# A spectral layer and two MLP layers on one core: who makes the low parts of the early weight pairs, and how the inverse transform's PSUM is cut

## The chip, the cores and the metric

The program runs on one core of one Trainium2 chip. Its time is the device time of one launch in microseconds, as the median of three runs. TensorE (PE) does the matrix products, VectorE (DVE), ScalarE (ACT) and GpSimd (POOL) the elementwise work, SyncE (SP) and POOL issue the DMAs.

## The reference

```python
X = np.fft.rfft(x, axis=1)                       # x: 2 x 3008 x 256
Yr = Xr @ w_r - Xi @ w_i + b_r
Yi = Xr @ w_i + Xi @ w_r + b_i
Y = soft_threshold(Yr, 0.01) + 1j * soft_threshold(Yi, 0.01)
x = np.fft.irfft(Y, n=3008, axis=1).reshape(6016, 256)
for w_in, w_out in ((moe_w_in, moe_w_out), (moe2_w_in, moe2_w_out)):
    h = x @ w_in                                 # 6016 x 2048
    x = (h * sigmoid(c * h)) @ w_out             # c = 1.702, then 1
```

The weights of the two MLP layers are float64 in memory. The kernel reads them as raw 64-bit words and makes float32 values of them on the chip.

## The kernel before

The program has four stages, one after the other on PE. **Forward** (16 tiles, `psf`): the input is folded into sums and differences and multiplied by cosine and sine matrices. **Middle** (12 tiles, `psm`): the complex product with `w_r` and `w_i`, then the threshold. **Inverse** (16 tiles, `psi`): for each parity q of the output index, each batch b and t = 0 to 3, the coefficients times a matrix. **MLP**: two layers, six blocks of 1024 (the last 896) tokens, eight groups each.

In the middle and in the MLP a float32 product is made of three products of a faster type: a number is cut into a high part (a cast) and a low part (the number less its high part), and high x high, high x low and low x high are added. `split` (L98) does this for weights: ACT casts, and POOL or DVE subtracts. For the middle's own input, `xsplit` (L470) makes the low part `xl` in another way: ACT writes minus the number in the faster type (L476), and a DMA issued by POOL adds the number onto it (L477). DMAs that add can be issued by POOL alone in this program.

**Weight pairs.** The weights come in 32 pairs of 128-row slices, in the order of `WEIGHTS` (L33): in 0 to 5, out 0 to 3, then out 4, in 6 and so on. One `tick` (L251) takes each pair one step on. It loads a pair (`raw`, one buffer, 512 KB), turns the bits of another (one operation on ACT, five on DVE, `cv_bits`, L159), sends the DMA that adds the two halves of the number (`cv_a<-cv_c`, L227), and places the one before that: `place_in` (L192) makes four sums on DVE in `tmp` (one buffer) and splits 384 and 512 columns; `place_out` (L183) splits 512. Ticks stand at listed steps: forward tiles 6, 9, 12, middle tiles 2, 6, 10, inverse tiles 1, 4, 7, 10; after that one in most MLP groups.

**Inverse.** Tiles t = 0, 1 of a (q, b) go into `rt`, tiles t = 2, 3 are added to and subtracted from it (L627, L628), and `inv_out` (L636) folds four times into `yt`, the MLP's input. Each tile has two PSUM banks, one for each half of the 128 + 128 channels; the four banks of one pool hold t = 0, 1 and the four of the other t = 2, 3. For q = 0, tiles t = 0, 1 are built of an even and an odd part: ACT copies the odd one to `eo` (L611, one buffer), and DVE makes sum and difference (L619, L374).

**Order.** In the inverse PE's instructions stand in the order of the code, and those of the other engines are put in order when the program is built, by a planned timeline; so are all engines' in the first MLP group. In the forward stage POOL and SP keep the order of the code, in the middle SP. Every engine runs its queue in order: an instruction that waits holds what is behind it.

Of the kernel before, what the change touches and what calls it, by code (L numbers as in the profile page):

```python
# [56 lines left out]
def spectral_mlp_kernel(ctx, tc, xin, mfwd, minv, wc, bias, w_in1, w_out1, w_in2, w_out2, outT):  # L57
# [101 lines left out]
    def cv_bits(raw):  # L159
# [875 lines left out]
```

## Time and profile before

| what | value |
|---|---|
| median of three runs | 1178.72 us (1176.81 to 1180.5) |
| the profiled execution: its own time, span | 1181.88 us, 1179.8 us |
| PE, PEld, DVE, ACT, POOL busy | 98%, 80%, 54%, 65%, 42% of the span |
| granted TensorE clock, mean | 0.998 of full speed |
| chain that ended last | 72% PE, 5% ACT, 2% DVE |

A busy PE is not PE at its peak, since its matmuls overlap. What counts is where it stands still, and for whom. A row of a timeline gives the start from the span's start, the length, the engine, the line of the kernel, the operation, output <- inputs and their shapes, the count, and in brackets the idle time ahead with the instruction that ended it. SP and POOL's DMA rows are the issue, not the transfer.

### The profile page before, as it was taken

How to read it: one execution, taken by the hardware profiler on the slowest of the kernel's cores; microseconds unless marked ns; L12 is line 12 of the kernel's file. 1: busy time of each engine (PE TensorE's matmuls, PEld its weight loads, DVE VectorE, ACT ScalarE, POOL GpSimd, SP SyncE). 2: the span in 40 equal slices, each digit the busy share in tenths (PEclk: the TensorE clock that was granted, in tenths of full speed). 3: DMA queues.
4: the chain of work that ended last, by engine and by line, in shares of the span. 5: the costliest groups of instructions: out<-in, count | busy, mean ns of one | idle time of the engine just before them, and what ended most of it. 6: DMA issues, size and time to landing. Idle time of an engine off the chain costs nothing.

```text
span 1179.8 us, 14452 instructions
## 1 busy us (share of the span) xinstructions
PE 1157.4 (98%) x5036; PEld 940.4 (80%) x5036; DVE 632.7 (54%) x976; ACT 761.3 (65%) x1437; POOL 499.9 (42%) x421
## 2 busy tenths in 40 slices
PE   7999989999999999999999999999999999999998
PEld 4758866788888888888889978878888888888897
DVE  7857998666456465565564553432532623524422
ACT  2465633678667667677667776666765765766655
POOL 2353532454444444444436755333333333433333
PEclk9999999999999999999999999999999999999999
DMA  7568332231221221121120100000000000000000
GB/s 267 181 135 229 54 72 54 55 80 28 54 72 36 54 72 28 45 72 37 54 63 28 54 18 19 1 37 1 1 37 1 20 17 1 36 1 1 36 1 32
DMA packets 33610, 61.35 MB, mean 52 GB/s; under 512 B 3073, under 2 KB 12289, under 8 KB 33538
## 3 DMA queue, kind: packets, MB, share of 16 engines
q1 hardware_dynamic: 25730, 46.28, 11.6%
q0 software_dynamic: 7808, 14.16, 6.9%
q8 instruction: 39, 0.64, 0.2%
q14 instruction: 33, 0.27, 0.1%
HBM read 35.92 MB, written 10.35 MB: 39 GB/s over the span
## 4 chain that ended last, share of the span: by engine, by line
PE 72%; ACT 5%; DVE 2%; issue 1%; DMA 0%; POOL 0%; DVEq 0%; ACTq 0%; POOLq 0%
PE o L727 38%; PE x L755 34%; ACT yt L758 2%; ACT g L760 1%; ACT x L674 1%; DVE x L681 1%; ACT yt L774 0%; DVE yt L776 0%; DVE yt L731 0%; DVE yt L797 0%; ACT yt L791 0%; DMA cv_a<-cv_c 0%; ACT yt L789 0%; ACT yt L731 0%; ACT wi L99 0%
## 5 line engine op out<-in xcount | busy, mean ns | idle before, releaser
L765 POOL TENSOR_TENSOR g<-yt,g 128x512 fp32r<-128x512 f32 (+1 forms) x282 | 361.3, 1294 | 531.6 <-PE x L755 364.3
L727 PE MATMUL o<-g,wo 128*128 128x512 f32 (+1 forms) x2304 | 561.0, 386 | 0.9 <-POOL g L765 0.9
L755 PE MATMUL x<-x,wi 128*128 128x512 f32 (+1 forms) x2016 | 501.7, 387 | 5.4 <-ACT yt L791 2.0
L727 PEld LDWEIGHTS o<-g,wo 128*128 128x128 f32 x2304 | 432.4, 188 | 83.6 <-POOL g L765 1.2
L755 PEld LDWEIGHTS x<-x,wi 128*128 128x128 f32 x2016 | 376.0, 188 | 86.0 <-ACT yt L774 5.6
L758 ACT ACTIVATE yt<-yt 128x512 f32<-128x512 f32 (+1 forms) x288 | 179.1, 622 | 257.8 <-DVE yt L797 209.9
L760 ACT CAST g<-yt 128x512 fp32r<-128x512 f32 (+1 forms) x384 | 234.4, 612 | 11.8
L797 DVE TENSOR_TENSOR yt<-yt,x 128x512 f32<-128x512 f32 (+1 forms) x96 | 64.7, 674 | 212.9 <-PE x L755 212.6
L776 DVE TENSOR_TENSOR yt<-yt,x 128x512 f32<-128x512 f32 (+1 forms) x96 | 64.8, 675 | 168.7 <-ACT yt L774 165.9
L765 DVE TENSOR_TENSOR g<-yt,g 128x512 fp32r<-128x512 f32 (+1 forms) x102 | 72.7, 713 | 77.8 <-ACT g L760 77.8
L344 PE MATMUL psf<-m,xf 128*128 128x376 f32 (+2 forms) x208 | 61.1, 456 | 6.4 <-DVE xf L303 6.1
L681 DVE TENSOR_TENSOR x<-yt,x 128x512 fp32r<-128x512 f32 (+1 forms) x46 | 47.8, 1038 | 36.1 <-ACT x L674 36.1
L800 DVE TENSOR_TENSOR yt<-yt,x 128x512 f32<-128x512 f32 (+1 forms) x96 | 64.7, 674 | 0.0
L344 PEld LDWEIGHTS psf<-m,xf 128*128 128x128 f32 x208 | 39.2, 199 | 27.6 <-DVE xf L303 7.3
L774 ACT COPY yt<-x 128x512 f32<-128x512 f32 (+1 forms) x96 | 54.7, 570 | 5.9 <-issue 3.6
L758 ACT ACTIVATE yt<-x 128x512 f32<-128x512 f32 (+1 forms) x96 | 56.1, 584 | 2.1 <-PE x L755 2.1
L344 PE MATMUL psi<-m,f 128*128 128x376 f32 (+3 forms) x208 | 52.1, 406 | 4.3 <-DVE rt L374 4.3
L791 ACT COPY yt<-x 128x512 f32<-128x512 f32 (+1 forms) x96 | 55.8, 581 | 0.8 <-PE x L755 0.8
L789 ACT COPY yt<-x 128x512 f32<-128x512 f32 (+1 forms) x96 | 54.8, 571 | 0.8 <-PE x L755 0.8
L344 PEld LDWEIGHTS psi<-m,f 128*128 128x128 f32 x208 | 37.2, 194 | 17.8 <-DVE rt L374 5.5
L227 POOL DMA_DIRECT2D cv_a<-cv_c x32 | 27.8, 870 | 24.7 <-DVE cv_c L174 14.2
L384 ACT COPY xt<-psf 128x128 f32<-128x128 f32 (+2 forms) x96 | 18.6, 282 | 28.6 <-PE psf L344 28.5
(99 smaller groups left out, 817.8 us busy)
## 6 DMA issues: line engine op xcount, KB each, us to landing
raw<-in_wi SPq DMA_DIRECT2D x32, 256.0 KB, 3.2
cv_a<-cv_c POOLq DMA_DIRECT2D x32, 256.0 KB, 3.3
raw<-in_wo SPq DMA_DIRECT2D x16, 512.0 KB, 3.4
raw<-in_x SPq DMA_DIRECT2D x12, 512.0 KB, 4.8
xl<-xt POOLq DMA_DIRECT2D x20, 256.0 KB, 7.6
out_t<-yt SPq DMA_DIRECT2D x20, 256.0 KB, 2.0
m<-in_mf SPq DMA_DIRECT2D x4, 564.0 KB, 5.3
m<-in_mi SPq DMA_DIRECT2D x4, 564.0 KB, 10.5
```

What stands on the lines that cost most here:

```text
L344: nc.tensor.matmul(ps, hi[:, c : c + P], m[:, k, :w], start=i == 0, stop=i == last)
L681: E('xl1' if l else 'xl0' if i == 0 else 'xl', k).tensor_sub(lo, src, r32(hi))
L727: nc.tensor.matmul(acc[h, mm], st, mv, start=first and k == 0, stop=last and k == 2)
L755: nc.tensor.matmul(ps, st, mv, start=first and m == 0, stop=m == 2, skip_group_check=True)
L758: nc.scalar.activation(g, g if src is None else src, func)
L760: nc.scalar.copy(gh, g)
L765: eng.tensor_sub(gl, g, r32(gh))
L776: nc.vector.tensor_add(y1, y1, Y)
L789: nc.scalar.copy(y2, Z)
L791: nc.scalar.copy(y3, X)
L797: nc.vector.tensor_add(y2, y2, X)
L800: nc.vector.tensor_add(y3, y3, Z)
```

## The change

- `split` gets a third way, `"D"`: ACT writes minus the number, POOL issues a DMA that adds the number, ACT casts the high part. `window` picks it for every pair that a tick places up to the last inverse tile (`outs[1]` is set behind it).
- Ticks stand at forward tiles 5, 8, 10, 13 (one more), middle tiles 3, 6, 9 and inverse tiles 0, 2, 5, 8. Pairs in 4 and later wait in `held` until the middle stage's buffers are closed; out pairs until inverse tile 5 (`po`).
- A tile of the inverse is one PSUM tile of two banks, four of them, in a pool of its own. ACT's copies and DVE's L627 and L628 take both halves in one instruction (L621, L641, L642 of the changed kernel).
- All folds of the threshold's result (`thf`, L530) are on DVE; one in four was on POOL.
- The buffer `a` of a conversion has three copies, and the weights fetched in the MLP use them too, where `ld` had one.

The entries that changed in the two tables of numbers are `thf`, `tf`, `tm`, `ti`, and the new `po`.

```diff
     def split(hi, lo, src, hi_eng=None, lo_eng=None):
+        if lo_eng == "D":
+            nc.scalar.mul(lo, src, -1.0)
+            nc.gpsimd.dma_start(out=lo, in_=src, accum_op=ALU.add)
+            nc.scalar.copy(hi, src)
+            return
...
-        a = cv_p.tile([P, 2 * CU], F32, tag="a", name="cv_a")
+        a = cv_p.tile([P, 2 * CU], F32, tag="a", name="cv_a", bufs=3)
...
     def window(k, done, now=False):
-        for u, a in done:
+        ready, held[:] = held + list(done), []
+        for u, a in ready:
+            if u[0] == "in" and u[2] >= NPR // 2 and not wib_p or u[0] == "out" and not outs[0]:
+                held.append((u, a))
+                continue
+            early = "D" if not now and not outs[1] else None
             if u[0] == "in":
-                sums, puts = place_in(u[1], u[2], a, E('pil', u[2]), sums_tmp)
+                sums, puts = place_in(u[1], u[2], a, early or E('pil', u[2]), sums_tmp)
...
-                place_out(u[1], u[2], a, E('pol', u[2]))
+                place_out(u[1], u[2], a, early or E('pol', u[2]))
...
-        a = cv_p.tile([P, 2 * CU], F32, tag="a" if kind == "in" else "ld", name="cv_ld", bufs=2 if kind == "in" else 1)
+        a = cv_p.tile([P, 2 * CU], F32, tag="a", name="cv_ld", bufs=3)
...
+    closed("ps1", "ps0")
+    psi_p = opened("psi", bufs=4, space=PS)
...
-        out = [bank(t // 2, "psi") for _ in range(2)]
+        pair = psi_p.tile([P, 2, 512], F32, tag="psi", name="psi")
+        out = [pair[:, x] for x in range(2)]
...
-        for mm in range(2):
-            r, a = row(rt[0], mm, t - 2, n), row(ac[0], mm, t - 2, n)
-            nc.vector.tensor_add(a, r, ps[mm][:, :n])
-            nc.vector.tensor_sub(r, r, ps[mm][:, :n])
+        r, a = rows(rt[0], t - 2, n), rows(ac[0], t - 2, n)
+        nc.vector.tensor_add(a, r, ps[:, :, :n])
+        nc.vector.tensor_sub(r, r, ps[:, :, :n])
...
+                outs[0] = step >= N('po')
...
+    outs[1] = True
     inv_post(*prev)
...
+    closed("psi")
+    ps_p[:] = [opened(f"ps{i}", bufs=4, space=PS) for i in range(2)]
```

The order of the instructions follows from the code and the planned timeline. Three places show it.

**POOL ahead of the middle's first split product.** `wi_` are the buffers of the placed in pairs, `xl<-xt_100` is the first low part that PE needs in the middle (its third tile). Before:

```order
L100 TENSOR_TENSOR wi_776<-cv_a,wi_776 128x384
L227 DMA cv_a<-cv_c 128x512
L100 TENSOR_TENSOR wi_776<-tmp,wi_776 128x512
L100 TENSOR_TENSOR wi_1012<-cv_a,wi_1012 128x384
L100 TENSOR_TENSOR wi_1012<-tmp,wi_1012 128x512
L227 DMA cv_a<-cv_c 128x512
L477 DMA xl<-xt_100 128x512
```

Now:

```order
L101 DMA wi_603<-cv_a 128x384
L101 DMA wi_603<-tmp 128x512
L232 DMA cv_a<-cv_c 128x512
L101 DMA wi_854<-cv_a 128x384
L101 DMA wi_854<-tmp 128x512
L101 DMA wi_1040<-cv_a 128x384
L232 DMA cv_a<-cv_c 128x512
L101 DMA wi_1040<-tmp 128x512
L487 DMA xl<-xt_100 128x512
```

Four in pairs are placed ahead of it (`wi_514` is further up) where there were three, and POOL's subtractions there have become DMAs. `tmp` has one buffer, and it is now read by a DMA: the next pair's sums wait until that DMA has landed.

**DVE in the inverse, second batch of q = 0.** L619 and L374 (now L634 and L384) read the tiles t = 0 and t = 1 whose banks PE needs again for q = 1; the numbers tell the tiles apart. Before:

```order
L619 TENSOR_TENSOR rt_1451<-psi_1401,eo_1452 128x2x2x95
L664 TENSOR_TENSOR tmp_1527<-yt_1325 128x512
L374 TENSOR_TENSOR rt_1451<-psi_1401,eo_1452 128x4x94
L665 TENSOR_TENSOR yt_1325<-yt_1325 128x512
L627 TENSOR_TENSOR ac_1480<-rt_1451,psi_1456 128x377
L681 TENSOR_TENSOR x_1604<-tmp_1527,x_1603 128x512
L627 TENSOR_TENSOR ac_1480<-rt_1451,psi_1457 128x377
L619 TENSOR_TENSOR rt_1451<-psi_1441,eo_1466 128x2x2x95
L628 TENSOR_TENSOR rt_1451<-rt_1451,psi_1456 128x377
L683 TENSOR_TENSOR tmp_1527<-yt_1325,tmp_1527 128x512
L170 TENSOR_SCALAR cv_c_1489<-cv_c_1489 128x512
L628 TENSOR_TENSOR rt_1451<-rt_1451,psi_1457 128x377
```

The next row there is L374 on `psi_1441`. Now:

```order
L634 TENSOR_TENSOR rt_1469<-psi_1444,eo_1470 128x2x2x95
L678 TENSOR_TENSOR tmp_1556<-yt_1349 128x512
L384 TENSOR_TENSOR rt_1469<-psi_1444,eo_1470 128x4x94
L679 TENSOR_TENSOR yt_1349<-yt_1349 128x512
L641 TENSOR_TENSOR ac_1514<-rt_1469,psi_1492 128x2x377
L642 TENSOR_TENSOR rt_1469<-rt_1469,psi_1492 128x2x377
L695 TENSOR_TENSOR x_1610<-tmp_1556,x_1609 128x512
L634 TENSOR_TENSOR rt_1469<-psi_1460,eo_1501 128x2x2x95
L175 TENSOR_SCALAR cv_c_1482<-cv_c_1482 128x512
L697 TENSOR_TENSOR tmp_1556<-yt_1349,tmp_1556 128x512
L384 TENSOR_TENSOR rt_1469<-eo_1501,psi_1460 128x4x94
```

The same work stands there in nearly the same order; two pairs of halves have become one instruction each, and the conversion's operation (L170, now L175) is still in it.

**DVE from the last inverse tile into the MLP.** The L648 rows (now L662) are the last `inv_out`, L776 (now L794) is the first sum of the MLP. Before:

```order
L627 TENSOR_TENSOR ac_1627<-rt_1600,psi_1619 128x376
L628 TENSOR_TENSOR rt_1600<-rt_1600,psi_1619 128x376
L627 TENSOR_TENSOR ac_1627<-rt_1600,psi_1620 128x376
L628 TENSOR_TENSOR rt_1600<-rt_1600,psi_1620 128x376
L648 TENSOR_TENSOR yt_1325<-ac_1627 128x2x376 x2
L648 TENSOR_TENSOR yt_1325<-rt_1600 128x2x376
L776 TENSOR_TENSOR yt_1325<-yt_1325,x_1645 128x512
L648 TENSOR_TENSOR yt_1325<-rt_1600 128x2x376
```

Now:

```order
L641 TENSOR_TENSOR ac_1630<-rt_1607,psi_1623 128x2x376
L642 TENSOR_TENSOR rt_1607<-rt_1607,psi_1623 128x2x376
L662 TENSOR_TENSOR yt_1349<-ac_1630 128x2x376 x2
L662 TENSOR_TENSOR yt_1349<-rt_1607 128x2x376 x2
L794 TENSOR_TENSOR yt_1349<-yt_1349,x_1651 128x512
```

The first sum has moved behind the fourth fold, and the last tile's fold is one wide instruction that starts only when both halves are there.

## Rows read from the trace of the kernel before

**Rows 1.** The waits of PE over the whole span: total us, times, longest

```profile
PE psi L344 <- DVE rt L374: 4.3, 2, 3.7
```

**Rows 2.** Windows: length, PE, PEld, DVE, ACT, POOL busy, clock, DMA share, GB/s

```profile
171.00:174.00 3.00, 2.55 (x6) 1.52 (x7) 3.00 (x7) 0.00 (x0) 0.00 (x0) 0.73 0.00 0
174.00:177.00 3.00, 3.00 (x8) 1.66 (x7) 3.00 (x6) 0.62 (x1) 0.00 (x0) 0.70 0.00 0
```

**Rows 3.** Timeline of PE in the inverse: start, us, line, tiles, idle before

```profile
160.10 3.02 PE L344 MATMUL psi<-m,f 128*128 128x190 f32 x12
163.71 4.06 PE L344 MATMUL psi<-m,f 128*128 128x376 f32 x12 [0.59 <-DVE rt L374]
171.45 26.59 PE L344 MATMUL psi<-m,f 128*128 128x376 f32 x78 [3.68 <-DVE rt L374]
```

**Rows 4.** Timeline of DVE from the end of the middle stage on

```profile
142.98 1.47 DVE L172 SCALAR_TENSOR_TENSOR cv_a<-raw,cv_c 128x512 uint32<-128x512 uint32 x1
144.37 1.48 DVE L518 SCALAR_TENSOR_TENSOR th<-sd,th 128x512 f32<-128x512 f32 x1
146.71 0.28 DVE L202 TENSOR_TENSOR tmp<-cv_a 128x128 f32<-128x128 f32 x1
146.91 1.37 DVE L203 TENSOR_TENSOR tmp<-cv_a 128x128 f32<-128x128 f32 x1
163.12 0.54 DVE L374 TENSOR_TENSOR rt<-psi,eo 128x376 f32<-128x376 f32 x1
163.57 2.46 DVE L665 TENSOR_TENSOR yt<-yt 128x512 f32<-128x512 f32 x1
168.99 1.49 DVE L170 TENSOR_SCALAR cv_c<-cv_c 128x512 f32<-128x512 f32 x1
170.86 0.53 DVE L374 TENSOR_TENSOR rt<-eo,psi 128x376 f32<-128x376 f32 x1
192.82 0.43 DVE L173 TENSOR_SCALAR cv_c<-cv_a 128x512 uint32<-128x512 uint32 x1
```

**Rows 5.** Timeline of POOL in the same stretch

```profile
143.85 1.45 POOL L100 TENSOR_TENSOR wi<-cv_a,wi 128x384 fp32r<-128x384 f32 x1
157.19 3.20 POOL L648 TENSOR_TENSOR yt<-rt 128x376 f32<-128x376 f32 x2 [4.11 <-issue]
163.53 1.94 POOL L100 TENSOR_TENSOR wo<-cv_a,wo 128x512 fp32r<-128x512 f32 x1
```

**Rows 6.** Timeline of DVE, two halves apart and two wide folds

```profile
181.64 1.00 DVE L627 TENSOR_TENSOR ac<-rt,psi 128x376 f32<-128x376 f32 x2
199.19 1.79 DVE L648 TENSOR_TENSOR yt<-ac 128x752 f32<-128x752 f32 x2
```

**Rows 7.** Start of the split products: timelines of ACT, POOL, PE

```profile
74.68 1.20 ACT L476 ACTIVATE xl<-xt 128x512 fp32r<-128x512 f32 x2
...
75.65 1.74 POOL L477 DMA_DIRECT2D xl<-xt  x2 [0.84 <-ACT xl L476]
...
83.56 0.50 PE L499 MATMUL psm<-wh,xl 128*128 128x512 f32 x1 [1.46 <-DMA xl<-xt]
```

**Rows 8.** The same stretch by windows, as rows 2

```profile
75.00:80.00 5.00, 5.00 (x13) 2.28 (x12) 1.12 (x1) 5.00 (x11) 3.68 (x5) 1.00 0.94 226
```

**Rows 9.** DMA issues of the page: count, KB, median us to landing

```profile
cv_a<-cv_c POOLq DMA_DIRECT2D x32, 256.0 KB, 3.3
xl<-xt POOLq DMA_DIRECT2D x20, 256.0 KB, 7.6
```

**Rows 10.** Start of the first layer: timelines of DVE, ACT, PE

```profile
198.15 0.55 DVE L627 TENSOR_TENSOR ac<-rt,psi 128x376 f32<-128x376 f32 x1 [0.77 <-PE psi L344]
201.75 0.68 DVE L776 TENSOR_TENSOR yt<-yt,x 128x512 f32<-128x512 f32 x1
...
202.47 0.63 ACT L758 ACTIVATE yt<-yt 128x512 f32<-128x512 f32 x1 [0.32 <-DVE yt L776]
...
205.35 1.29 PE L727 MATMUL o<-g,wo 128*128 128x512 f32 x5
```

More of the change, by code (lines that the diff above doesn't have):

```diff
@@ L12 @@
-NUM = dict(li=[5, 6, 7, 8], n32=2, nhb=6, tf=[5, 9, 13], tm=[1, 3, 5, 7, 9, 11], ti=[0, 2, 4, 6, 8, 10, 12, 14, 14, 15, 15], kb=[2] * 8, kr=1, fa=3, fe=2, pm=0, nf=4, lvb=6, ddb=8, ivb=1, eob=1, fsb=6, f1=3, f2=0, fm=[7, 8, 9], fi=[1, 1, 2, 2], pre=13, pre2=1, yd=3, psh=0, ie=[12], xp=[1, 3, 4, 5], xq=[1, 2, 2], xs=5, nw=4, xi=[14, 14, 15, 15], xsi=13, rw=2, ca=4, cc=2, tb=1, tmn=1)
+CFG = {'lv0': 'V', 'lv': 'VVVVVPVVVVVP', 'dd0': 'VPVVPPPPPVVP', 'dd': 'VVVVVVVVVVPV', 'ths': 'VVVVPV', 'thf': 'V', 'ivf': 'VVVPVVVV', 'cva': 'P', 'pol': 'PPPP', 'pil': 'P', 'mvl': 'PVVP', 'xl': 'V', 'xse': 'V', 'gl': 'VPPPPPPP', 'tf': [5, 8, 10, 13], 'tm': [3, 6, 9], 'ti': [0, 2, 5, 8], 'kb': [0, 1, 1, 1, 1, 1, 1, 0], 'kr': [0, 1, 0, 1, 0, 1, 1, 0], 'fa': 3, 'xp': [2, 4, 4, 5], 'xq': [1, 4, 1], 'xs': 4, 'xi': [11, 12, 13, 15], 'xsi': 9, 'ca': 4, 'tl': True, 'fwd': 'Pool,SP', 'rest0': 'all', 'rest1': 'all', 'last1': 'all', 'inv': 'PE', 'mid': 'SP', 'last0': 'all', 'thm': 'A', 'gl0': 'PVPVVVPV', 'gl2': 'PPPPPPPP', 'gl3': 'PPPPPPPV', 'xl0': 'V', 'xl1': 'V', 'pre': 14, 'pre2': 0, 'yd': 6, 'lvb': 6, 'mlp': 'none', 'pr': 'VVVP', 'pf': 'PV', 'eo': '0010', 'n32': 2, 'xa': 4, 'nhb': 6, 'ddb': 6, 'mlp1': 'all', 'mlp2': 'all'}
@@ L14 @@
+NUM = dict(po=5, li=[5, 6, 7, 8], n32=2, nhb=6, tf=[5, 9, 13], tm=[1, 3, 5, 7, 9, 11], ti=[0, 2, 4, 6, 8, 10, 12, 14, 14, 15, 15], kb=[2] * 8, kr=1, fa=3, fe=2, pm=0, nf=4, lvb=6, ddb=8, ivb=1, eob=1, fsb=6, f1=3, f2=0, fm=[7, 8, 9], fi=[1, 1, 2, 2], pre=13, pre2=1, yd=3, psh=0, ie=[12], xp=[1, 3, 4, 5], xq=[1, 2, 2], xs=5, nw=4, xi=[14, 14, 15, 15], xsi=13, rw=2, ca=4, cc=2, tb=1, tmn=1)
 DEF = dict(pr="V", pf="V", lv0="V", lv="VPP", dd0="VVVVVP", dd="VPV", mpl="PV", ths="VP", thf="VVPP", fsl="VP", ivf="PPVV", cva="P", pol="P", pil="P", mvl="V", xl="PPVVPPP", xl0="PPVVPPP", xl1="PPVVPPP", xse="VP", gl="P", gl0="P", gl2="P", gl3="P", wcl="V", thc="V", thm="V")
@@ L209, in place_in @@
         )
-    wib_p = []
+    wib_p, held, outs = [], [], [False, False]
     spare = []
@@ L582, in inv_mm @@
                     product(out[eo][:, mm * CU : mm * CU + w], tiles, m, blocks, w, cs * D + mm * P)
-            return out
+            return pair
         for mm in range(2):
@@ L590, in inv_mm @@
                 product(out[mm][:, :188], tiles, m, ((1 - cs, 2), (2, 3)), 188, c)
-        return out
+        return pair
     rt, ac = {}, {}
@@ L597, in row, with rows @@
         return x[:, t * RW + mm * 378 : t * RW + mm * 378 + n]
+    def rows(x, t, n):
+        return x[:, t * RW : (t + 1) * RW].rearrange("p (m c) -> p m c", m=2)[:, :, :n]
     def inv_post(q, b, t, ps):
@@ L604, in inv_post @@
         if t < 2 and not split_sums("i", q, 0):
-            for mm in range(2):
-                nc.scalar.copy(row(rt[0], mm, t, n), ps[mm][:, :n])
+            nc.scalar.copy(rows(rt[0], t, n), ps[:, :, :n])
             return
@@ L609, in inv_post @@
             w = mshape("i", q, 0)[1]
-            ev, od = by_half(ps[0]), by_half(iv_p.tile([P, 2 * CU], F32, tag="eo", name="eo", bufs=N("eob")))
-            nc.scalar.copy(od[:, :, :w], by_half(ps[1])[:, :, :w])
+            ev, od = by_half(ps[:, 0]), by_half(iv_p.tile([P, 2 * CU], F32, tag="eo", name="eo", bufs=N("eob")))
+            nc.scalar.copy(od[:, :, :w], by_half(ps[:, 1])[:, :, :w])
             add, sub = nc.vector.tensor_add, diff(t)
@@ L624, in inv_post @@
             ac[0] = iv_p.tile([P, 2 * RW], F32, tag="ac", name="ac")
-        for mm in range(2):
-            r, a = row(rt[0], mm, t - 2, n), row(ac[0], mm, t - 2, n)
-            nc.vector.tensor_add(a, r, ps[mm][:, :n])
-            nc.vector.tensor_sub(r, r, ps[mm][:, :n])
+        r, a = rows(rt[0], t - 2, n), rows(ac[0], t - 2, n)
+        nc.vector.tensor_add(a, r, ps[:, :, :n])
+        nc.vector.tensor_sub(r, r, ps[:, :, :n])
         if t == 3:
```

1 line of the change is left out of this document (removed).

## The prediction, made before the changed kernel was run

> **What bounds the kernel.** I read the table of engines first: PE is busy for 98% of the span, no other engine for more than 65%. The matrix work stays as it is, so only the time in which PE stands still, or runs at the lower clock, can come or go. The list of PE's waits is therefore the second view, and there one group touches the edited lines: psi on DVE's L374, 4.3 us in two waits, the longer one of 3.7 [rows 1]. The timeline of PE puts them into q = 1 of the inverse: 0.59 us ahead of 163.71, 3.68 us ahead of 171.45 [rows 3]. The windows behind the longer one show a granted clock of 0.73 and 0.70 for three us each, a mixture of 2.4 and 1.2 GHz; what is lost there is 3 x 0.27 + 3 x 0.30 = 1.7 us [rows 2]. So this place costs 4.3 + 1.7 = 6.0 us, and nothing else the change touches costs PE as much: 1.46 us at the start of the middle's split products [rows 7], and the way into the first layer [rows 10].
>
> The timeline of DVE tells why L374 is late. PE is not waiting for a chain but for a full DVE, on which some instructions take far longer than their own kind elsewhere. A sum of 128x512 takes 0.68 at 201.75 [rows 10], a TENSOR_SCALAR of that size 0.43 at 192.82, and a row of 128x128 0.28 at 146.71 [rows 4]. Against these, the rows at 142.98, 144.37, 146.91, 163.57 and 168.99 are 0.79, 0.80, 1.09, 1.78 and 1.06 us too long, 5.5 us together [rows 4]. Beside several of them POOL has a TENSOR_TENSOR in flight: L100 at 143.85 and 163.53, L648 at 157.19 for comparison [rows 5]. I take it that two such instructions side by side stretch each other.
>
> **Part 1, the inverse.** The change takes L100 off POOL there (POOL issues a DMA instead) and L530 too. I let the five stretches go: 2.7 of the 5.5 lie ahead of the first L374 (142.98, 144.37, 146.91), the others between the first and the second. Added to DVE: one fold of the threshold, 0.68 us by the sum of that size [rows 10], 0.7 in round. Merged halves: two halves take 1.00, one instruction of two halves 1.79 / 2 = 0.90, by the wide folds [rows 6]; 0.1 for each of some six pairs ahead of the second L374 is 0.6, and 0.4 ahead of the first. New waits: a pair's low parts need three more ACT instructions than before, of 1.20 / 2 = 0.60 each [rows 7], and `eo`'s copy can stand behind them: 0 to 1.8 us, and I take half, 0.9, since DVE has other work for part of it.
>
> First L374: it ended at 163.12 + 0.54 = 163.66 [rows 4]. Now 163.66 - 2.7 + 0.7 - 0.4 + 0.9 = 162.3. Second: 171.39 - 5.5 + 0.7 - 0.6 + 0.9 = 166.9. When does PE want them? Twelve matmuls of 376 columns take 4.06 us [rows 3]. Before, a tile's halves waited apart: six of the twelve in the row at 160.10 are already the first half of tile t = 0, so they began about 2.0 us ahead of its end at 163.12, at 161.1 [rows 3]. In a two-bank tile both halves wait for the last reader, so the tile starts at 162.3, 1.2 late. It ends its twelve matmuls at 166.4, and t = 1 starts at 166.9, 0.5 late. So 1.7 us of the 4.3 stay, 2.6 go. With no stall near 3.7 us left, I expect the clock to stay up: another 1.7. **-4.3 us.** Bounds: the place costs nothing (-6.0); no stretch goes and the ACT wait is full, which makes the first tile 163.66 + 0.7 - 0.4 + 1.8 = 165.8, 4.7 late, and the second 173.3 against 169.9, 3.4 late: 8.1 - 4.3 = +3.8.
>
> **Part 2, the start of the middle.** Four in pairs instead of three are placed ahead of `xl_100`. That is one ACT instruction of 0.60 and two POOL issues of 1.74 / 2 = 0.87 more ahead of it [rows 7]. And `tmp`, one buffer, is now read by a DMA, so the fourth pair's sums wait until the third pair's DMA has landed: 3.3 us by the DMA that adds 256 KB in a conversion [rows 9]. If ACT's queue stands behind that, L476 at 74.68 starts 3.3 us later. On the other side the landing is in question: from the first issue at 75.65 to PE's start at 83.56 there are 7.9 us [rows 7], in a stretch with the DMA engines 94% busy [rows 8]; that is a queue of transfers, and the one step later finds it partly drained. Drained to the 3.3 of rows 9, the whole wait of 1.46 goes (-1.5); not drained, +3.3. I take the middle, **+0.9**. Upper bound: landing, two issues and the ACT instruction all add up, 3.3 + 1.74 + 0.60 = 5.6, and PE's wait of 1.46 + 5.6 = 7.1 is longer than the 3.7 behind which the clock fell, so 1.7 more: +7.3.
>
> Here rules of the notes can be weighed. The median landing of the `xl` transfers is 7.6 us [rows 9]. The Trainium skill ("DMA: Bandwidth & Descriptors", section "Anatomy of one DMA - SWDGE (gpsimd) path") fits a DMA issued by POOL with 2.0 us and its bytes at 436 GB/s, which would be an estimate of 2.6 us for 256 KB; by it the wait would go wholly and the sum would stand 2.4 us lower. The trace has 3.3 and 7.6, so the measurement decides. One rule speaks against this change: the row of the stretch from 75 to 80 shows DVE with one instruction in 1.12 us [rows 8], and the Trainium skill ("SBUF - State Buffer", section "SBUF: two separate sides") says that DVE in some of its modes keeps POOL from writing a DMA's descriptors. By it each added issue could wait for one DVE instruction; two of 0.43 would be 0.9 us more. The trace shows issues of 0.87 beside a DVE that is seldom busy there, and bears out neither.
>
> **Part 3, into the first layer.** The last tile is read by L627 and L628. Before, the first half's pair lay beside PE's last matmuls, and from 198.15 (PE's last product is done) to the folds at 199.19 there were 1.04 us [rows 6, 10]. Now two wide instructions start there: 1.79 by the wide folds [rows 6], +0.75. Then four folds, where the fourth stood behind the first sum of the MLP: +0.90. The sum at 201.75 comes 1.65 later, and ACT's L758 waits for it (0.32 idle) [rows 10]. PE's products of this group hang on that chain: **+1.7**. Bounds: 0, if PE has other work meanwhile, and +2.9, if ACT's copies that have changed places with L758 add two times 0.63 [rows 10].
>
> **Part 4, the rest** I cost at nothing. The forward's fourth tick puts a load ahead of the last x loads on SP; the tiles in between hide it, and without that cover it is one landing, 3.3 us. The three buffers of `a` and the use of them in the MLP take nothing off PE's path that the waits show.
>
> **Sum:** -4.3 + 0.9 + 1.7 = -1.7 us. The profiled execution took 1181.88 us, so 1180.2 on its scale; it stood 3.2 us above the median of the runs, 1178.72, which gives **1177.0**.
>
> **Rivals.**
> (a) *The inverse's place costs nothing, and neither do the others.* If DVE has no stretch left and no wait for ACT, the first L374 ends near PE's want and both stalls go with the clock loss: -6.0; the middle's landing shortens as much as its issue is late, and PE has o products of its own at the MLP's start: 0. That is 1172.7. For it: PE's two waits end on DVE alone, and 5.5 us of stretch are more than 4.3. Against it: the whole-tile wait of part 1.
> (b) *The middle turns into the bound.* `xl_100` lands so late that PE's stall there passes 3.7 us: +7.3 - 4.3 + 1.7 = +4.7, 1183.4. It decides from a landing 2.2 us later than now (3.7 - 1.5). For it: PE already waits for just this transfer [rows 7]. Against it: the drained queue [rows 8].
> (c) *The change does not do what it says.* DVE's order in the inverse still has a conversion's operations between L634 and L384, and the ticks there are as many as before; the stretches may be of the load on memory by any neighbour, and a DMA is one. Then 4.3 + 1.7 stay, and the sum is 0 + 0.9 + 1.7 = +2.6: 1181.3. Against it: the stretched rows stand beside POOL's sums [rows 4, 5].
>
> **Numbers.** Forecast 0.45, (a) 0.32, (b) 0.12, (c) 0.11. A measurement of this kernel can tell 0.3%, 3.5 us, from no change. (a) is faster (0.32), and of the forecast's own spread the part with the middle's gain of 1.5 and a cheaper MLP start, 0.08: faster 0.40. (b) is slower (0.12), and 0.02 of (c): slower 0.14. The rest, 0.46, is within it. The best sum of the bounds is -6.0 - 1.5 + 0 = -7.5, 1171.2; the range leaves out its very end and (b): 1171.5 to 1182.0.
>
> **What would show it.** In the profile after: the waits of PE psi on DVE below 2 us, and no clock below 1 behind them; DVE's rows between 142 and 170 at 0.43 and 0.68 beside POOL's DMA issues; PE's wait for `xl` by its length, 0 to 7; the first L794 later than the last psi product by 1.65 us more than the 3.7 of now (201.75 less 198.04, where rows 3 end). The prediction is wrong if the stretches stay without POOL's sums, if a wait on a DMA stands in front of L384, or if the middle's wait passes 3.7 us.

## The result, and the profile after

The changed kernel takes 1188.8 us (median of six runs, 1186.56 to 1192.38), the kernel before 1180.04 in the same runs: a ratio of 1.0075, 95% interval 1.0051 to 1.0099. It is slower, by 8.8 us, where 1.7 us less were forecast, and it lies outside the range (1171.5 to 1182.0).

The list of PE's waits after, the groups that have no like in [rows 1] or [rows 7] or have grown. The columns are total us, times, longest:

```profile
PE psf L354 <- DMA m<-in_mf: 2.8, 1, 2.8
PE x L773 <- DVE yt L815: 2.5, 2, 1.9
PE psi L354 <- ACT wo L100: 2.3, 1, 2.3
PE psm L509 <- DMA xl<-xt: 2.0, 1, 2.0
PE x L773 <- DVE rt L642: 1.5, 1, 1.5
PE psm L509 <- ACT xh L490: 1.4, 1, 1.4
PE psi L354 <- DVE rt L384: 1.3, 1, 1.3
```

A wait is not yet time lost, since the next stage may have had slack. So I set the two traces against each other: PE issues 5036 matmuls in both, and for each the start in one trace less the start in the other is how late it is. The table has the growth of that lateness by stage (us, worked out from the two traces; the marks stand at 48.8, 89.7, 145, 197, 221 and 313 us of the kernel before). Behind it, the medians of the runs; the experiments' rows are used below.

| kernel | forward | start of middle | rest of middle | inverse | start of layer 1 | layer 1, first block | rest | all | median us |
|---|---|---|---|---|---|---|---|---|---|
| after | 2.6 | 0.5 | 1.7 | -0.2 | 1.7 | 2.6 | -1.3 | 7.7 | 1188.8 |
| forecast | 0 | 0.9 | 0 | -4.3 | 1.7 | 0 | 0 | -1.7 | 1177.0 |
| 1 | -0.2 | 6.4 | 2.6 | 0.0 | 1.8 | 2.7 | -0.6 | 12.7 | 1193.1 |
| 2 | 1.2 | 0.5 | 0.0 | -4.4 | 1.8 | 2.6 | -1.3 | 0.5 | 1184.3 |
| 3 | 2.3 | 1.0 | 0.7 | 0.6 | -0.7 | 3.9 | -1.4 | 6.3 | 1188.7 |
| 4 | 4.6 | -1.6 | 1.7 | 0.9 | 1.8 | 2.7 | -0.2 | 9.9 | 1189.0 |
| 5 | 2.0 | 5.1 | 0.0 | -3.6 | 2.5 | 0.0 | -0.6 | 5.5 | 1187.0 |
| 6 | 2.6 | -0.3 | 0.0 | -0.9 | 1.9 | 2.6 | -0.6 | 5.4 | 1186.9 |
| 7 | 1.3 | 6.7 | 0.0 | 1.4 | 1.8 | 2.7 | -1.4 | 12.5 | 1194.0 |
| 8 | -0.4 | 0.2 | 7.3 | -2.7 | 2.4 | 0.0 | -0.2 | 6.6 | 1189.1 |
| 9 | 5.7 | -1.8 | 0.0 | -4.4 | 1.8 | 2.7 | -1.3 | 2.8 | 1185.4 |
| 10 | 0.5 | -0.5 | 4.3 | -4.4 | 1.8 | 2.7 | -1.3 | 3.1 | 1184.9 |
| 11 | -0.4 | -1.8 | 3.1 | -0.6 | -0.6 | 0.0 | -0.5 | -0.7 | 1181.6 |
| 12 | 5.9 | -1.3 | 0.0 | -2.6 | 1.8 | 2.7 | 0.6 | 7.0 | 1188.7 |
| 13 | -0.3 | 6.9 | 2.1 | -3.4 | 2.5 | 0.0 | -1.3 | 6.4 | 1187.4 |
| 14 | 0.1 | 6.4 | 1.8 | -1.2 | -0.6 | 0.0 | -1.3 | 5.3 | 1189.4 |
| 15 | 0.4 | 6.9 | 1.8 | -3.3 | 2.6 | 0.0 | 0.6 | 9.0 | 1189.3 |
| 16 | 0.3 | -1.6 | 1.1 | 5.0 | -0.6 | 0.0 | 0.7 | 4.9 | 1186.6 |
| 17 | 0.4 | -1.8 | 0.0 | 0.7 | -0.4 | 0.0 | -1.0 | -2.1 | 1182.8 |
| 18 | 0.8 | -0.2 | 0.0 | 2.7 | 2.6 | 0.3 | -0.5 | 5.8 | 1187.3 |

The kernel before has 1180 to 1181 us in all these comparisons. A row compares one profiled execution with that of the kernel before, which took 1181.88 us, 1.8 us more than the median of its six runs. The profiled executions of 2, 14 and 17 took 2.3, 2.4 and 3.4 us less than their medians, that of 4 took 2.5 us more. So a row tells where time goes, and the medians tell how much it is in all. 5, 6, 7, 12 and 18 have a single run each.

**Forward.** SP's timeline after (the rows are the issues, x the count):

```profile
27.30 0.47 SPq L158 DMA_DIRECT2D raw<-in_wi  x1
36.61 0.37 SPq L157 DMA_DIRECT2D raw<-in_wi  x1
37.02 0.47 SPq L158 DMA_DIRECT2D raw<-in_wi  x1
37.54 1.42 SPq L287 DMA_DIRECT2D raw<-in_x  x3
39.05 2.88 SPq L127 DMA_DIRECT2D m<-in_mf  x2
```

```profile
49.50 20.56 PE L354 MATMUL psf<-m,xf 128*128 128x376 f32 x80 [2.76 <-DMA m<-in_mf]
86.72 0.50 PE L509 MATMUL psm<-wh,xl 128*128 128x512 f32 x1 [2.01 <-DMA xl<-xt]
```

The second fence is PE's. The second weight load stood on SP from 27.8 to 36.6 us, for its one buffer, and with it the x loads and the matrix behind it; they came out in one burst, and the matrix was late by 2.76 us. The start of the split products, at 83.56 before [rows 7], is at 86.72.

**A late load in front of ACT.** Timelines of ACT, DVE and SP after, at 97 to 122 us (the last row takes three issues together, the first of them at 107.38):

```profile
120.98 0.66 ACT L170 ACTIVATE cv_c<-raw 128x512 f32<-128x512 f32 x1 [8.64 <-DMA raw<-in_wo]
```

```profile
121.67 0.43 DVE L175 TENSOR_SCALAR cv_c<-cv_c 128x512 f32<-128x512 f32 x1 [7.75 <-ACT cv_c L170]
```

```profile
96.69 3.99 SPq L132 DMA_DIRECT2D m<-in_mi  x6
107.38 61.83 SPq L161 DMA_DIRECT2D raw<-in_wo  x3
```

A conversion's first operation stands in ACT's queue where the planned timeline expected its load. The load was issued at 107.38, behind six matrices, and ACT waited 8.6 us for it; what stands behind it on ACT are the evacuations of the middle's tiles. (Before, the load was issued at 104.78, also behind six matrices, but these had gone out from 91.20 on, and ACT waited 3.5 us.) PE lost 1.4 us at once. But DVE, idle for 7.8 us, was now behind. It still had not caught up at the end of the stage. DVE's sum for the last middle tile and PE's first product of the inverse, after and then before:

```profile
149.39 0.68 DVE L521 TENSOR_TENSOR sd<-us,psm 128x512 f32<-128x512 f32 x1
145.18 5.36 PE L354 MATMUL psi<-m,f 128*128 128x192 f32 x32
```

```profile
141.72 0.68 DVE L511 TENSOR_TENSOR sd<-us,psm 128x512 f32<-128x512 f32 x1
140.41 6.01 PE L344 MATMUL psi<-m,f 128*128 128x192 f32 x36
```

DVE is 4.2 us behind PE there; before, it was 1.3 us.

**Inverse.** PE's rows there, the clock behind them (0.66 of full speed over 5 us, a mixture of 2.4 and 1.2 GHz), and two rows of DVE:

```profile
157.53 6.08 PE L354 MATMUL psi<-m,f 128*128 128x192 f32 x36 [1.34 <-DVE rt L384]
170.39 32.25 PE L354 MATMUL psi<-m,f 128*128 128x376 f32 x96 [2.29 <-ACT wo L100]
```

```profile
170.00:175.00 5.00, 4.61 (x9) 2.58 (x10) 4.81 (x9) 2.44 (x5) 2.59 (x3) 0.66 1.08 227
```

```profile
166.11 1.20 DVE L178 TENSOR_SCALAR cv_c<-cv_a 128x512 uint32<-128x512 uint32 x1
169.75 0.54 DVE L384 TENSOR_TENSOR rt<-psi,eo 128x376 f32<-128x376 f32 x1
```

The second wait is put down to ACT, but L384, which reads that tile's banks, ends at 170.29, 0.1 us ahead of PE: it is DVE again. The stretched rows of [rows 4] are gone. Two other rows are still long, L178 (1.20 us) and a fold (L658, 1.74), beside POOL's two folds at 163.82 (3.21 us); they were as long before (L173 1.20, L644 1.73), beside the same folds. So the forecast's mechanism is at work, and yet nothing is gained in all.

**Start of the first layer.** DVE after, and PE, to compare with [rows 10]:

```profile
202.75 0.94 DVE L641 TENSOR_TENSOR ac<-rt,psi 128x752 f32<-128x752 f32 x1 [1.81 <-PE psi L354]
203.72 0.94 DVE L642 TENSOR_TENSOR rt<-rt,psi 128x752 f32<-128x752 f32 x1
204.58 1.78 DVE L662 TENSOR_TENSOR yt<-ac 128x752 f32<-128x752 f32 x2
206.28 1.79 DVE L662 TENSOR_TENSOR yt<-rt 128x752 f32<-128x752 f32 x2
207.99 0.68 DVE L794 TENSOR_TENSOR yt<-yt,x 128x512 f32<-128x512 f32 x1
```

```profile
204.81 3.67 PE L773 MATMUL x<-x,wi 128*128 128x512 f32 x15 [1.47 <-DVE rt L642]
233.47 2.34 PE L773 MATMUL x<-x,wi 128*128 128x512 f32 x9 [1.86 <-DVE yt L815]
```

From DVE's first row to the sum there are 5.24 us, before 201.75 - 198.15 = 3.60: 1.64 more, where 1.65 were worked out.

### The profile page after: what moved, and what is told of

It reads as the page before. It is cut to its first block, busy times and chain, and to the rows that moved or that the text cites. A ratio compares the mean times of both kernels' runs of the same rounds, so it can differ in the third digit from the quotient of the medians.

```text
span 1187.4 us, 14439 instructions
## 1 busy us (share of the span) xinstructions
PE 1155.2 (97%) x5036; PEld 939.3 (79%) x5036; DVE 623.9 (53%) x965; ACT 767.9 (65%) x1448; POOL 484.6 (41%) x416
## 4 chain that ended last, share of the span: by engine, by line
PE 70%; ACT 4%; DVE 2%; issue 1%; DMA 0%; POOL 0%; DVEq 0%; ACTq 0%; POOLq 0%
PE o L745 37%; PE x L773 33%; ACT yt L776 1%; ACT g L778 1%; DVE x L695 0%; ACT x L688 0%; ACT yt L792 0%; DVE yt L815 0%; DVE yt L794 0%; DVE yt L749 0%; DMA cv_a<-cv_c 0%; ACT yt L809 0%; ACT yt L807 0%; ACT yt L749 0%; DVE cv_c L178 0%
## 5 line engine op out<-in xcount | busy, mean ns | idle before, releaser
L776 ACT ACTIVATE yt<-yt 128x512 f32<-128x512 f32 (+1 forms) x288 | 179.0, 622 | 260.9 <-DVE yt L815 210.9
L815 DVE TENSOR_TENSOR yt<-yt,x 128x512 f32<-128x512 f32 (+1 forms) x96 | 64.7, 674 | 215.8 <-PE x L773 215.0
L794 DVE TENSOR_TENSOR yt<-yt,x 128x512 f32<-128x512 f32 (+1 forms) x96 | 64.8, 675 | 167.2 <-ACT yt L792 164.7
L776 ACT ACTIVATE yt<-x 128x512 f32<-128x512 f32 (+1 forms) x96 | 56.1, 585 | 3.4 <-PE x L773 3.4
L170 ACT ACTIVATE cv_c<-raw 128x512 f32<-128x512 f32 x32 | 21.5, 671 | 29.8 <-DMA raw<-in_wo 16.4
```

The lines of the kernel that those rows point to most:

```text
L776: nc.scalar.activation(g, g if src is None else src, func)
L794: nc.vector.tensor_add(y1, y1, Y)
L815: nc.vector.tensor_add(y2, y2, X)
```

## The experiments

All but 11 and 16 to 18 are edits of the changed kernel. The runs of a number are its row in the table.

**1.** The first forward tick.

```diff
-'tf': [5, 8, 10, 13]
+'tf': [6, 8, 10, 13]
```

> The changed kernel with forward ticks at tiles 6, 8, 10, 13 instead of 5, 8, 10, 13; still four of them, the same number of pairs converted. On SP this puts the second weight load behind the last three x loads, as it stood before the change. Theory (order on SP): in the changed kernel SP stands from 27.8 to 36.6 us at that weight load, because raw has one buffer, and the three x loads and two matrices behind it come out in one burst; so here PE's wait of 2.8 us for the DMA of m at 46.7 us goes to 0 and the middle starts about 2.7 us earlier; total about -2.7. Rival (load on the DMAs: a fourth pair is simply more traffic in the forward stage): the wait stays above 2 us, total within 0.7 of the changed kernel.

Ratio to before 1.0105 (1.0083 to 1.0127). The theory on SP's order holds: the wait is gone, forward -0.2. But the total rose by 4 us:

```profile
87.11 0.79 PE L509 MATMUL psm<-wh,xl 128*128 128x512 f32 x1 [5.20 <-DMA xl<-xt]
```

```profile
88.00:90.00 2.00, 2.00 (x6) 1.51 (x6) 1.73 (x3) 0.42 (x1) 0.46 (x1) 0.50 1.12 203
```

PE comes to the same transfer earlier and starts no earlier (87.11). The forward stall had been hidden under that landing; as one stall of 5.2 us it also took the clock down to 1.2 GHz (0.50 behind it).

**2.** The loads of inverse matrices.

```diff
-li=[5, 6, 7, 8]
+li=[5, 9, 10, 11]
```

> The changed kernel with the last three loads of inverse matrices at middle tiles 9, 10, 11 instead of 6, 7, 8, so the weight pair's load is issued ahead of them. Theory (a late DMA in front of ACT): ACT's first operation of a conversion, which waits 8.6 us for its raw load at 112 to 121 us, waits under 3; PE's wait of 1.4 us on xh at 120 us goes, DVE's 7.8 us of idle time go, DVE is no longer behind at the end of the middle, and PE's waits in the inverse (0.25, 1.3 and 2.3 us) lose at least 2.5 us together; total about -4 to -5. Rival (the inverse's waits come from the two-bank tiles and the folds on DVE, not from the late start): only the 1.4 us at 120 go, the inverse's waits stay above 3 us together; total about -1.5.

4.5 us less than the changed kernel; ratio to before 1.0036 (1.0023 to 1.0048). ACT, DVE and PE at the start of the inverse, and the clock after PE's one remaining wait there (1.9 us, ahead of 164.84):

```profile
110.13 0.67 ACT L170 ACTIVATE cv_c<-raw 128x512 f32<-128x512 f32 x1 [2.54 <-DMA raw<-in_wo]
```

```profile
142.66 0.68 DVE L521 TENSOR_TENSOR sd<-us,psm 128x512 f32<-128x512 f32 x1
142.15 6.01 PE L354 MATMUL psi<-m,f 128*128 128x192 f32 x36
```

```profile
164.00:168.00 4.00, 3.16 (x10) 2.01 (x11) 3.96 (x7) 2.25 (x5) 3.05 (x4) 1.00 1.06 231
168.00:171.00 3.00, 3.00 (x11) 1.80 (x10) 2.94 (x7) 2.30 (x5) 0.86 (x1) 1.00 1.12 200
```

ACT waits 2.5 us instead of 8.6, the rest of the middle loses nothing, DVE is 0.5 us behind instead of 4.2, and the inverse gains 4.4 us: what the forecast had, with 1.9 us of wait left where it had 1.7, and the clock up.

**3.** One-bank tiles: `bank(t // 2, "psi")` twice, L621, L641 and L642 by halves, no pool `psi`.

> The changed kernel with the inverse's tiles as two one-bank tiles again, and ACT's copies and DVE's sums by halves; all else as changed. Theory (the inverse is late for other reasons; at its end the two-bank tile costs): PE's waits in the inverse stay within 1 us of the changed kernel's 3.9 together, and PE's 1.5 us wait on L642 at the start of the first MLP layer goes, with the first sum of the layer some 0.7 us earlier; total about -1 to -2. Rival (whole tiles are what keeps PE waiting in the inverse): the inverse's waits fall by over 2 us; total -3 or better. The other way: without the merged instructions DVE has about 0.6 us more to do ahead of the second wait, which makes it +0.6.

The layer's start falls from 1.7 to -0.7, the inverse rises by 0.8; the first block loses 1.3 more, with the clock down there. Ratio 1.0068 (1.0045 to 1.0091): no difference to the changed kernel. PE's waits in the inverse are 4.2 us, so whole tiles were not what held it.

**4.** The folds.

```diff
-'thf': 'V'
+'thf': 'VVVP'
```

> The changed kernel with one fold in four of the threshold's result on POOL again. Theory (DVE is late from the wait at 112 to 121 us on): a middle tile costs DVE 4.1 us with all folds and about 3.5 with a part of them on POOL, so what is left of the lateness at the end of the middle falls by 1 to 2 us, and PE's waits in the inverse by about as much: total -1 to -2. Rival (DVE's instructions beside POOL's sums are stretched, so the folds on POOL cost as much as they save): no change in the inverse's waits beyond 0.5 us; total within 0.7.

1188.95 us; the inverse's waits are 4.1 us in all. The rival holds: moving the folds is worth nothing here.

**5.** Three forward ticks.

```diff
-'tf': [5, 8, 10, 13]
+'tf': [6, 9, 12]
```

> The changed kernel with forward ticks at tiles 6, 9, 12, as before the change: one pair fewer on the way ahead of the middle's first low part xl_100. Theory (the fourth pair sets the landing of xl_100, and the forward stall of 2.8 us was hidden under it): both the forward wait on m and the surplus at the middle's start go; the first product with xl starts within 1 us of the kernel before, which is 2 to 3 us earlier than in the changed kernel (86.7 us), without a fall of the clock there. Rival (the low parts by DMA, whatever the count of pairs, delay ACT and the transfers): forward wait gone, but PE waits over 4 us for xl and starts at 86 us or later, as with four ticks of which the first stands at 6 (87.1 us).

The forward wait is gone (its 2.0 arose in the first 17 us), but PE starts xl at 90.1 us after a wait of 5.0 us: the weight load found its buffer free sooner, and SP sent the six matrices at 79 to 83 us, among the xl transfers, whose issue to landing rose to 9.5 us and more. ACT's late load is not there (0.7 us), and the inverse gains 3.6. The first block's 2.6 us are gone: they come with the fourth tick. With it, DVE has the four sums of a pair (L207 to L210, 231.79 to 232.81 after) ahead of the L815 that PE waits for; with three ticks they are not there.

**6.** A second buffer for the sums, in the pool `wc`, in turn with `tmp`.

> The changed kernel with a second buffer for the four sums of an in pair, in turn with the first, up to the end of the middle stage. Theory of the prediction (the sums wait until the DMA that reads tmp has landed, and ACT's queue with xl_100's first operation stands behind): ACT's wait of 2.6 us on L210 at 78 us goes, xl_100 is issued 2 us earlier than 81.8 us, PE's wait for it falls from 2.0 us to under 0.7. Rival (the transfers ahead of xl_100 decide): it is issued earlier but lands within 1 us of 86.7 us, since its landing grows from 4.9 to 6 us or more.

The rival holds: xl_100 is issued 3.4 us earlier (78.35) and lands 0.75 us earlier (85.92), after 7.6 us. The transfers decide. ACT still waits 8.2 us for the raw load, and though PE loses nothing there, the inverse gains 0.9 only.

**7.** No low parts by DMA.

```diff
-early = "D" if not now and not outs[1] else None
+early = None
```

> The changed kernel with the low parts of early pairs by POOL's subtraction again, all else as changed. Theory (the low parts by DMA cost at the middle's start, in transfers and in waits on tmp): xl_100 lands at least 1.5 us earlier than 86.7 us. In the inverse, where POOL's sums stretched DVE's instructions before the change, DVE's stretches come back: three rows or more between 145 and 180 us over 1.2 us where 0.43 or 0.68 are usual, and PE's waits there grow from 3.9 to over 5 us. Rival (the stretches and the start come from elsewhere): neither moves by more than 1 us.

xl_100 lands 2.7 us later (89.4), not earlier: the theory on that falls, and PE's wait there (5.6 us) is put down to DVE's L475. In the inverse, DVE and POOL:

```profile
173.13 4.39 DVE L176 TENSOR_SCALAR cv_c<-cv_c 128x512 uint32<-128x512 uint32 x1
```

```profile
173.20 4.02 POOL L105 TENSOR_TENSOR wo<-cv_a,wo 128x512 fp32r<-128x512 f32 x3
```

The stretches are back (a 0.42 us operation takes 4.39 beside three of POOL's), and the inverse loses 1.4 us; PE's waits there don't pass 3.9. The run takes 5.2 us more than the changed kernel, most of it at the start of the middle (6.7 against 0.5): by this one run the low parts by DMA are a gain in the changed kernel, and not what slows it.

**8.** 2 and 5 together.

> The changed kernel with forward ticks at 6, 9, 12 and the last matrices loaded at middle tiles 9, 10, 11: the forward edit and the edit of the second experiment together. Theory (two places, each with its own cause: pairs ahead of xl_100, matrices ahead of a raw load that ACT waits for): the gains add, -2.5 and -4.5 against the changed kernel's 1188.8 us: 1181 to 1183 us, so no difference from the kernel before. If the inverse then also gains its 4 us against the kernel before, 1178. Rival (one late thing moves another): less than 5 us in total.

1189.1: the rival holds. The start of the middle is clear, and the matrices, sent at 96 to 100 us even so, then meet the later xl transfers: 7.3 us in the rest of the middle. In the inverse the wait of 1.9 us is that of 2, but the clock falls behind it (0.57 from 171 to 175 us), and the inverse gains 2.7 instead of 4.4.

**9.** All matrices late.

```diff
-li=[5, 6, 7, 8]
+li=[8, 9, 10, 11]
```

> The changed kernel with all four loads of inverse matrices at middle tiles 8 to 11 (5 to 8 in it): none of them among the transfers ahead of xl_100, none ahead of the raw load that ACT waits for at 112 us. Theory (matrices and weight pairs collide at two places: the landing of xl_100, and the raw load): the first product with xl starts at 84.7 us, when PE is there after its forward stall, instead of 86.7 us (-2.0); the later stall goes as in the second experiment (-4.5); together 1182 to 1183 us. Rival (the low parts' own DMAs and the weight loads fill the transfers ahead of xl_100 even so): no better than the second experiment, 1184.

1185.4. No wait for xl at all; but in the profiled run PE waited longer in the forward stage (3.6 us on DVE's L313, and the clock fell), so this shows the mechanism and not the sum. The inverse gains 4.4 again.

**10.** 9, and the first tick at 6.

> As the ninth experiment, and the first forward tick at tile 6. Theory: the forward stall of 2.8 us goes, and with the matrices out of the way xl_100 lands by 83 us, so this time the middle doesn't take it back: 1179 to 1181 us, 2 to 3 us below the ninth. Rival (four pairs in the forward stage are too many for ACT and the transfers, whatever the matrices do): PE waits for xl over 4 us, the clock falls, and it is slower than the ninth.

1184.9, ratio 1.0043 (1.0026 to 1.0060). As in 8, forward and start of the middle are clear together (0.0), and the surplus moves on: PE waits four times, 4.5 us, for later xl transfers.

**11.** The `li` of 9 in the kernel before.

> The kernel before with its four matrix loads at middle tiles 8 to 11. Tells whether the late matrices are a gain of their own. Theory: the kernel before loses 1.5 us on xl_100 and no more than that to its transfers, so it gains at most 1.5 us at 82 us and up to 1 us of lateness ahead of the inverse: -1 to -2.5 us. Rival (its inverse waits, 4.3 us, also come from a late DMA ahead of ACT, which waits 3.5 us at 109 to 113 us): -4 or better.

1181.6, ratio 1.0013 (1.0003 to 1.0024): 1.8 gained at the start of the middle, 3.1 lost behind it, and PE's inverse waits stay at 3.9. Both theories are wrong.

**12.** 9, and the layer's PSUM pools in each other's place (`[::-1]`).

> The ninth experiment's kernel with the two PSUM pools of the MLP in each other's place, so that the first layer's first tiles lie where the inverse's t = 0 and 1 were. Theory (PE's wait of 1.5 us on L642 at 203 us is for the banks of the last whole tile): that wait goes; but the first sum of the layer waits for DVE's folds, so PE stands still 1 to 1.5 us longer behind it, and the layer's group ends within 0.5 us. Rival (the wait is on the path): the layer starts 1.5 us earlier and stays so.

The wait on L642 is gone, and a wait of 1.9 us on L794 stands in its place; the start costs 1.8 as before. The banks are not on the path, the folds are. In the inverse the wait is that of 9, 1.9 us, but the clock falls behind it, and the inverse gains 2.6 instead of 4.4.

**13.** 9 with `tf` [6, 9, 12] and `tm` [2, 6, 10].

> The changed kernel with the forward and middle ticks as before the change (6, 9, 12 and 2, 6, 10) and all matrices at middle tiles 8 to 11; the inverse's ticks, the low parts by DMA, the folds and the two-bank tiles as changed. Theory (the number of pairs on the way decides the early collisions, and the fifth conversion in the layer's first groups stands differently): no forward stall, under 1 us lost at the start of the middle, inverse 4 us shorter than in the kernel before, and PE's wait of 1.9 us on L815 near 231 us gone, so the first layer's start costs 2 to 3 us instead of 4: 1177 to 1180 us. Rival (the surplus in the layer comes from the two-bank tile alone, and the matrices collide with the later low parts of the middle): L815's wait stays, or the middle loses over 2 us: 1182 to 1185 us.

1187.4. L815's wait is gone and the inverse gains 3.4; but SP sent four loads of matrices at 79 to 83 us, and PE waited 6.0 us for xl. To write a load later in the code did not send it later here, since SP had nothing to wait for.

**14.** 13 with the edit of 3.

> As the thirteenth, with the inverse's tiles as two one-bank tiles again. DVE's fourth fold then stands behind the layer's first sum again, and ACT's copy of y3 ahead of the first gelu. Theory (the start of the first layer pays 2.5 to 3 us for the two-bank tile: whole last tile, four folds, ACT's order): the layer's first groups gain 2.5 to 3 us against the thirteenth, the inverse loses up to 1 us: about -2 against it. Rival (the start is bound elsewhere): within 0.7 us in the layer, so slower by what the inverse loses.

The start of the layer costs 3.1 us less than in 13 (-0.6 against 2.5), the inverse gains 2.2 less. So in the trace the two-bank tile in the whole inverse takes more in the layer than it gives before it. The medians don't show that: 14 takes 1189.4 us, 13 takes 1187.4, and the profiled execution of 14 is the fastest of its four. 3 against the changed kernel shows no difference either.

**15.** 13, with L641 and L642 of the last tile by halves.

> As the thirteenth, but L641 and L642 of the very last tile by halves; the order behind them (four folds, then the first sum) as in the changed kernel. Theory of the prediction (0.75 us of the start are the whole last tile): the first sum of the layer comes 0.7 us earlier and the layer with it, -0.7 against the thirteenth. Rival (a half of a two-bank tile is not released by itself, or the folds bind): no difference beyond 0.3 us in the trace.

The first half's sum still starts only when PE is done with both (1.81 us idle, as with whole tiles), and the start costs 2.6. The rival holds.

**16.** The kernel before with two-bank tiles for twelve tiles and one-bank tiles for the last four.

> The kernel before (its ticks, its low parts by POOL, its folds) with two-bank tiles and merged instructions for the inverse's first twelve tiles, and one-bank tiles for the last four. Theory (a two-bank tile is worth about 3 us in the inverse and costs 3 us at the start of the first layer, and the early stages of the kernel before are clear): the inverse gains 3 us, the order at the layer's start is that of the kernel before and costs nothing: -3, so 1176 to 1178 us where the kernel before has 1180. Rival (the inverse's gain needs the low parts by DMA, since POOL's sums beside DVE stretch it): PE's waits on DVE there stay above 3.5 us in all, total within 1 us of the kernel before.

Ratio 1.0043 (1.0027 to 1.0058). The layer's start is clear, as expected; the inverse loses 5.0, with one stall of 6.2 us:

```profile
165.19 3.26 DVE L171 TENSOR_SCALAR cv_c<-cv_c 128x512 uint32<-128x512 uint32 x1
```

```profile
165.35 2.80 POOL L100 TENSOR_TENSOR wo<-cv_a,wo 128x512 fp32r<-128x512 f32 x2
```

**17.** 16, and the low parts of pairs placed in the inverse by DMA.

> As the sixteenth, with the low parts by DMA for the pairs placed in the inverse alone. Theory (both parts are worth something): PE's waits in the inverse fall to 2 us or less in all and the clock stays up there; the inverse is 4 us shorter than in the kernel before: 1175 to 1177 us. Rival (the two-bank tiles have taken the whole gain): within 0.5 us of the sixteenth in the trace. The other way: ACT's three more instructions delay the copies to eo and PE waits longer than in the sixteenth.

The same place is clear:

```profile
165.41 0.42 DVE L175 TENSOR_SCALAR cv_c<-cv_c 128x512 f32<-128x512 f32 x1
166.80 0.43 DVE L176 TENSOR_SCALAR cv_c<-cv_c 128x512 uint32<-128x512 uint32 x1
```

The inverse is 4.3 us shorter than in 16. Ratio to before 1.0010 (0.9997 to 1.0023): no difference can be told. Waits of 2.3 and 2.7 us stay in the inverse, so the forecast's whole gain isn't had without the rest of the change.

**18.** The kernel before with two-bank tiles in the whole inverse.

> The kernel before with two-bank tiles in the whole inverse, as the change has them, and nothing else of the change. Theory: the inverse as in the sixteenth (-3 us), the start of the first layer 3 us later than in it: no difference from the kernel before in all. Rival (the layer's surplus comes with the changed ticks): as the sixteenth.

The layer's start costs 2.6 us, where 16 has -0.6: the surplus comes with the tiles alone. The inverse loses 2.7 (the 6.2 us stall is there too), so "no difference in all" was wrong.

No version that was run beats both kernels.

## Why the prediction was wrong, step by step

**What bounds the kernel**: right. PE's standing still, and what clock follows, makes up the difference.

**Part 1, the inverse (-4.3; measured -0.2).** The step that failed is the one that took DVE's time at the inverse's start from the kernel before: "now 163.66 - 2.7 + ..." lets DVE enter as early against PE as it did. It entered 2.9 us later (4.2 against 1.3), because of ACT's wait for a late load, which the prediction did not look for. Over the experiments that decides: where ACT waits 8.1 to 8.7 us, DVE is 2.5 to 4.5 us behind and the inverse brings -0.9 to 0.9 (after, 1, 4, 6); where ACT waits 0.7 to 5.8 us, DVE is 0.5 to 1.2 us behind and the inverse brings -2.6 to -4.4 (2, 5, 8, 9, 10, 12, 13, 15). Three edits touch the inverse itself: one-bank tiles bring 0.6 where ACT waits 8.3 us (3) and -1.2 where it waits 5.6 (14), and with POOL's subtractions the inverse loses 1.4 although DVE is only 1.2 us behind (7).

With the load in time the sum of part 1 holds, but only where the clock stays up: -4.4 in 2, 9 and 10, and -2.7 and -2.6 in 8 and 12, where the same 1.9 us of wait take it down. The terms fit less well than their sum. The first L384 is 162.2 by its own terms, not 162.3, which moves 0.1 us from one tile's lateness to the other's; and in 2 all 1.9 us of wait stand at the first tile, where 1.2 were put, and none at the second, where 0.5 were.

Its reason, that POOL's sums stretch DVE's instructions, is shown by 7, 16 and 17. The Trainium skill ("SBUF — State Buffer", section "SBUF: two separate sides") says of the ports which the two engines share that, with DVE in some of its modes, one engine has them for a whole instruction and the other waits. The trace agrees in that the DVE row of 3.26 us in 16 ends only behind POOL's 2.80. But its row begins first, at 165.19 against 165.35, and it waits out two instructions in a row, which the page would not lead one to expect.

**Part 2, the start of the middle (+0.9; measured 0.5).** Right by accident. The landing itself is 3.2 us later (86.7 against 83.5), at the end where the transfers are not drained (+3.3); PE arrived late as well, so little was seen. Rival (b) was nearer than its chance of 0.12: experiment 1, without the forward stall, has its 5.2 us and the lower clock. `tmp`'s landing, on which part 2 built, is real (ACT waits 2.6 us at 78 us) but worth 0.75 us (6). Nor do the low parts by DMA delay the landing: with POOL's subtractions it is later still (7). With the matrices out of the way it is 2.1 us earlier (84.59 in 9).

**Part 3, into the first layer (+1.7; measured 1.7).** Right in mechanism: the wide last tile and the fourth fold stand ahead of the first sum (12, 14), and the tiles alone bring the surplus (18). The exact size is in part luck, since with three forward ticks, or with the tiles alone, the same stage costs 2.4 to 2.6 (5, 8, 13, 15, 18).

**Part 4, the rest at nothing (measured 2.6 in the forward stage, 1.7 in the rest of the middle, 2.6 in the first block, -1.3 later).** Wrong. "The tiles in between hide it" named the cover but did not check it against SP's queue: what was moved ahead was a load that waits, so everything behind it came late and at once. And the fourth tick puts a pair's sums ahead of a sum that PE waits for, which the first block pays. Of the rest of the middle, 1.4 us are PE's wait behind ACT's late load.

**The numbers.** Slower had 0.14, and the range ended 6.8 us too low: every case was built on the stages that the diff touches, none on a load that comes late because other transfers are in its way.

## What to carry to other kernels

When a change moves DMA issues, write down for each queue what now stands behind an instruction that waits, and for each engine the instruction that waits for the moved load: ACT's one late conversion cost here, with what followed, about half of the loss (4.5 of 8.8 us, by the medians of experiment 2). Read a stall removed together with the next one: in experiment 1 the forward stall went and the sum got worse. And compare two traces by the lateness of the same instruction, stage by stage; the list of waits alone hides that DVE was behind.

## What was not expected of the hardware

The length of a stall alone does not tell whether the clock falls behind it. After 1.9 us in the inverse it stayed at 1.00 in 2, 9, 10, 13 and 15, and fell in 8 and 12. After 2.3 us it fell in the changed kernel (0.66 over 5 us), while after 2.8 us in its forward stage, and after 2.7 us in the inverse of 17, it stayed up. After 5.2 us it was at 0.50 (1). Two windows, with the columns of [rows 2]: in the changed kernel behind the wait that ends at 49.50, and in 12 behind the one that ends at 167.7:

```profile
50.00:53.00 3.00, 3.00 (x11) 1.79 (x10) 2.96 (x10) 2.06 (x7) 1.48 (x2) 1.00 0.95 322
```

```profile
168.00:172.00 4.00, 4.00 (x8) 2.07 (x8) 3.93 (x7) 1.55 (x4) 1.95 (x3) 0.57 1.04 243
```

What decides between them stays open here. The price does not: 12 and 9 differ by it alone in the inverse, -2.6 against -4.4, so one fall costs 1.8 us.

One DVE instruction can wait out several of POOL's in a row: 4.39 us beside three, 3.26 beside two, where it takes 0.42 alone.
